# Two of a head's four causal masks move from TensorE to GpSimd

## The chip, the cores and the metric

One NeuronCore of a Trainium2 chip runs the whole kernel. The metric is the device time of one execution in microseconds. The engines are named as the profile names them: PE (TensorE matmul), PEld (its weight loads), DVE (VectorE), ACT (ScalarE), POOL (GpSimd) and SP (SyncE, which issues the DMAs).

## The reference

Attention with 4 x 8 heads, 576 positions and 64 features per head, and then two dense layers on the 2304 x 512 result.

```python
scores = scale * np.matmul(q, k.transpose(0, 1, 3, 2))
causal = np.triu(np.ones((S, S), dtype=bool), k=1)
cum = np.cumsum(np.maximum(s, 0.0), axis=-1)
bias = -(cum[:, :, :, None] - cum[:, :, None, :])
scores = np.where(causal, -1000000000.0, scores + np.minimum(bias, 0.0))
attn = np.exp(scores - max); attn = attn / (sum + 1e-09); out = attn @ v
h = x @ w_in;  x = (h - np.tanh(h)) @ w_out                    # first layer, d_ff 2048
h = x @ w_in;  x = (h * np.clip(h + 3, 0, 6) / 6) @ w_out      # second layer, d_ff 2048
```

## The kernel before, in words

**Stages.** The attention of 32 heads (16 pairs) runs to about 198 us, the first dense layer to about 600 us, the second to the end.

**A pair of heads** (`heads`) loads q and k (`lq`, `lk`), and splits each into a rounded high part and a rest: ACT makes the high q (`q1`, L421) and the high k for the second operand (`k2`, L433), DVE casts k (`kh`, L430), and GpSimd makes the two rests (`ql`, L427, and `kl`, L437). PE multiplies high parts for an upper bound on each row's scores (`mx`, L481), DVE reduces that to a maximum (`rd`, L490), and the maximum goes back through DRAM as extra rows of the q operand.

**The scores of a head** (`scores`) are transposed: keys on the partitions, queries along the free axis. Five key tiles are packed into four PSUM banks, c = 0 to 3 (`CHUNKS`), 256, 320, 512 and 512 columns wide. The function `st` (L575) issues a bank's matmuls in the order of `STEPS[c]`: `h` multiplies the 128-row operand with the rests, `l` the 68-row operand with the high parts, the bias and the maximum, and `m` multiplies the bf16 identity `identb` with a bf16 mask tile `maskT`, which adds -8e9 where the key is later than the query. Banks 0, 2 and 3 have such an `m`, 128, 192 and 2 x 128 columns wide (`MASKS`). ACT then takes the exponential of the whole bank into an SBUF tile `pt` (`ex`, L578; two tiles for each c), and PE multiplies it with the values (`pv`, L605, four groups per head in the order c = 0 to 3). A row of ones in the values gives the sum of the exponentials.

**What sets the order.** Nothing is scheduled at run time. `Plan` is a list scheduler in the host code: each operation has an engine, an estimated duration (`mm_us`, `vec_us`), a priority (`PRIO` plus a term that grows with the head), and buffers; the plan's start times give the order in which each engine's instructions are issued, and each engine then runs its own list strictly in that order, with semaphores between them. Constants of the plan are the latency after an operation (`LAT`) and a model of the DMAs (`DMA_US`, `DMA_KB_US`, `ISSUE`). Operations marked `port` (DVE and GpSimd work on two SBUF operands or in a copy) aren't planned beside each other, and each such GpSimd operation gets a dependence on the last such DVE operation of the plan.

**Around it.** While attention runs, ACT and DVE also turn the first 6 of 16 packed weight blocks of the first layer from 64-bit words into two rounded float parts (`rounded` and `convert`, L748 to L779, priority `conv`); the other 10 follow after attention, when their buffers come free (`close`). After every fourth pair GpSimd multiplies the batch's outputs with the reciprocal sums (`no`, L673), the last batch on DVE. The first layer's matmuls are L830 and L861, those of the second L1122 and L1198.

Of the kernel before, what the change touches and what calls it, by code (L numbers as in the profile page):

```python
# [15 lines left out]
ALU = mybir.AluOpType  # L16
# [8 lines left out]
SP = 640  # L25
# [12 lines left out]
CHUNKS = [  # L38
    [(0, 0, 256, 0)],
    [(0, 256, 320, 0)],  # L40
    [(4, 512, 64, 0), (1, 128, 448, 64)],
    [(3, 384, 192, 0), (2, 256, 320, 192)],
]
CW = [256, 320, 512, 512]

MASKS = [(1, 64, 128), None, (1, 0, 192), (2, 64, 128)]

STEPS = ["h0 l0 m", "h0 l0", "h1 l1 h0 l0 m", "h1 h0 l1 l0 m"]

MAXT = [[(2, 384, 0), (4, 576, 384)], [(3, 512, 0)], [(1, 256, 0), (0, 128, 256)]]  # L50
TINY, HUGE = (float(np.array([b], np.uint32).view(np.float32)[0]) for b in (0x38000000, 0x47F00000))
# [6 lines left out]

PRIO = {
# [3 lines left out]
}  # L65

# [40 lines left out]

class Plan:  # L110
    LAT = {"PE": 0.30, "ACT": 0.05, "DVE": 0.09, "POOL": 0.09, "V": 0.0}
    DMA_US, DMA_KB_US, ISSUE = 1.6, 220.0, 0.55

    def __init__(self):
        self.ops = []
# [23 lines left out]
    def schedule(self):  # L139
        wait, ready = {}, {}  # L140
        free = {}
# [10 lines left out]
        while done < len(self.ops):  # L152
# [6 lines left out]
            while frees and frees[0][0] <= t:  # L159
                _, _, b = heapq.heappop(frees)  # L160
                b.pool.free.append(b.t)
            for e in wait:
                while wait[e] and wait[e][0][0] <= t + 1e-9:
                    _, i, o = heapq.heappop(wait[e])
                    heapq.heappush(ready[e], (o.prio, i, o))
            again = True
            while again:
                again = False
                for e in ready:
# [25 lines left out]
                    o = chosen  # L195
# [21 lines left out]
                            heapq.heappush(frees, (b.end, id(b), b))  # L217
                    for n in o.next:
                        n.left -= 1
                        n.ready = max(n.ready, o.end)  # L220
                        if n.left == 0:
                            heapq.heappush(wait[n.eng], (n.ready, order[n], n))
                            if n.ready <= t:
                                heapq.heappush(events, t)
# [3 lines left out]

def mm_us(n, f32=False):

    return (4 * n / 2.4 + 6) / 1e3 if f32 else max(0.1, (n / 2.4 + (13 if n > 128 else 5)) / 1e3)


def vec_us(n, ghz, fixed):
    return (n / ghz + fixed) / 1e3
# [3 lines left out]
def kernel(  # L239
# [10 lines left out]
    nc = tc.nc  # L250
    plan = Plan()
# [43 lines left out]
    def r(b):  # L295
        return late[b.t] if isinstance(b.t, str) else b.t
# [99 lines left out]

    T = PRIO["T"]
    alloc_prev = [None, None]
# [158 lines left out]
    def scores(h, hh, t0, b1, b2, vf, deps, lv, xp, xb, bt, sds):  # L557
        def st(c, b):
# [13 lines left out]

            mms = [step(x) for x in STEPS[c].split()]
            for i, (o, w, x) in enumerate(mms):
                nc.tensor.matmul(o, w, x, start=(i == 0), stop=(i == len(mms) - 1), skip_group_check=True)  # L575

        def ex(c, b, pt):
            nc.scalar.activation(r(pt), r(b)[:, 0 : CW[c]], AF.Exp, scale=0.125)  # L578

        exs, pts, sts = [], [], []  # L580
        for c in range(4):
            b, pt = Buf(banks), Buf(ptp[c])
            us = sum(2 * mm_us(n) for _, _, n, _ in CHUNKS[c]) + (mm_us(MASKS[c][0] * MASKS[c][2]) if MASKS[c] else 0)
            so = plan.op("PE", us, lambda c=c, b=b: st(c, b), deps, [b1, b2, b], t0 + PRIO["st"] + PRIO["dst"] * c, name=f"st{h}_{c}")
            sts.append(so)
            exs.append(plan.op("ACT", vec_us(CW[c], 1.2, 165), lambda c=c, b=b, pt=pt: ex(c, b, pt), [so], [b, pt], t0 + PRIO["ex"] + PRIO["dst"] * c, name=f"ex{h}_{c}"))
            pts.append(pt)
        st_done[h] = sts
        po = [Buf(banks, greedy=True) for _ in range(2)]
# [21 lines left out]
        for c in range(4):  # L611
            us = sum(mm_us(n, True) for _, _, _, n, _ in segments(c))
# [24 lines left out]
        sd = plan.dma(sd_, 2, [ov1], own, t0 + PRIO["sd"], name=f"sd{h}")  # L637
        batch_sd.setdefault(bt, []).append(sd)
        if hh:
            so = plan.dma(lambda: nc.sync.dma_start(xp()[64:128], r(sg)[0:D, :]), 147, [sds[0], ov1], own + [xb], t0 + PRIO["so"], name=f"so{h}")  # L640
# [680 lines left out]
```

## Time and profile before

| | us |
|---|---|
| median of 3 runs (957.64 to 961.81) | 960.91 |
| the profiled execution, its own time | 957.06 |
| its span, first to last instruction | 955.3 |
| PE busy | 933.0 |
| DVE busy | 672.8 |
| ACT busy | 464.9 |
| GpSimd busy | 161.2 |

A busy time is the time in which an engine had at least one instruction under way. Matmuls are pipelined, so what one of them costs is read from the distance between its start and the next one's start, not from its own duration. A timeline row merges neighbours of one group: its columns are start, length, engine, line, operation, tiles, shapes, how many instructions, and in brackets the idle time ahead and what ended it.

### The profile page before, as it was taken

What the parts mean: (1) busy time and instruction counts of PE and PEld (TensorE: products, weight loads), DVE (VectorE), ACT (ScalarE), POOL (GpSimd) and SP (SyncE); (2) the same over time, 40 slices, a digit from 0 to 9 for tenths busy, and PEclk for the clock granted to TensorE, in tenths of its full rate; (3) what the DMA queues carried; (4) which work ended last, traced back from release to release, by engine and by line L of the source; (5) the groups of instructions that cost most, each with busy time, mean ns of one, the idle gap of its engine ahead of it and who ended that gap; (6) DMA issues with size and microseconds to landing.
All of it is one profiled execution on the core that took longest, in us unless ns stands there. A gap on an engine that the chain in (4) does not pass through costs nothing.

```text
span 955.3 us, 14956 instructions
## 1 busy us (share of the span) xinstructions
PE 933.0 (98%) x5560; PEld 831.9 (87%) x5560; DVE 672.8 (70%) x1107; ACT 464.9 (49%) x714; POOL 161.2 (17%) x106
## 2 busy tenths in 40 slices
PE   3999999999999999999999999999999999999998
PEld 3777777778878888998888888999999999999997
DVE  7887778789988766685676834657776577764763
ACT  2677677754534443444344333444454444544441
POOL 8344755600000000012222222000000000000000
PEclk9999999999999999999999999999999999999999
DMA  5667786796236448555546681776886767877672
GB/s 121 189 176 186 212 208 204 186 331 208 98 128 223 176 156 282 177 179 197 198 155 207 228 292 46 244 229 208 250 307 228 232 199 258 298 235 223 210 224 97
DMA packets 70521, 195.91 MB, mean 205 GB/s; under 512 B 11634, under 2 KB 20338, under 8 KB 69168
## 3 DMA queue, kind: packets, MB, share of 16 engines
q1 hardware_dynamic: 70448, 194.95, 64.3%
q8 instruction: 44, 0.72, 0.3%
q14 instruction: 29, 0.24, 0.1%
HBM read 143.75 MB, written 44.09 MB: 197 GB/s over the span
## 4 chain that ended last, share of the span: by engine, by line
PE 92%; DVE 3%; DMA 2%; ACT 1%; issue 1%; SPq 0%; DVEq 0%; ACTq 0%
PE bank L830 20%; PE bank L861 20%; PE pair L1198 19%; PE pair L1122 18%; PE bank L605 8%; PE bank L575 5%; DVE junk L490 1%; PE wide L481 1%; DMA tq<-in_q_dram 1%; PE bank L481 1%; DMA Q<-mdram 0%; DMA rdram<-rb 0%; ACT w L778 0%; DVE K L430 0%; DVE f_w L1142 0%
## 5 line engine op out<-in xcount | busy, mean ns | idle before, releaser
L861 PE MATMUL bank<-gg,w 128*128 128x512 f32 (+1 forms) x960 | 234.3, 368 | 0.5 <-ACT gg L849 0.3
L830 PE MATMUL bank<-xx,w 128*128 128x512 f32 (+1 forms) x960 | 233.2, 368 | 0.0
L861 PEld LDWEIGHTS bank<-gg,w 128*128 128x128 f32 x960 | 170.1, 189 | 30.9 <-ACT gg L849 1.3
L830 PEld LDWEIGHTS bank<-xx,w 128*128 128x128 f32 x960 | 170.5, 188 | 30.4
L1122 PE MATMUL pair<-op_w,w 128*128 128x384 f32 x648 | 118.0, 334 | 0.6 <-DVE f_w L1142 0.6
L841 ACT ACTIVATE g<-bank 128x512 f32<-128x512 f32 (+1 forms) x80 | 44.5, 556 | 148.2 <-PE bank L830 124.9
L1198 PE MATMUL pair<-w,op_W 128*128 128x256 f32 x918 | 115.1, 283 | 0.0
L1122 PEld LDWEIGHTS pair<-op_w,w 128*128 128x128 f32 x648 | 112.4, 188 | 1.2 <-DVE f_w L1142 0.9
L1198 PEld LDWEIGHTS pair<-w,op_W 128*128 128x128 f32 x918 | 112.8, 192 | 0.0
L605 PE MATMUL bank<-pt,vf 128*66 128x320 f32 (+4 forms) x448 | 106.9, 360 | 0.3 <-ACT pt L578 0.3
L851 POOL TENSOR_TENSOR gg<-g,gg 128x512 fp32r<-128x512 f32 x32 | 47.5, 1486 | 345.0 <-ACT gg L849 307.8
L845 DVE TENSOR_TENSOR g<-bank,g 128x512 f32<-128x512 f32 (+1 forms) x80 | 50.8, 635 | 64.4 <-ACT g L841 63.7
L575 PE MATMUL bank<-Q,K 128*128 128x320 f32 (+9 forms) x384 | 88.7, 352 | 1.6 <-ACT stage L628 1.1
L575 PEld LDWEIGHTS bank<-Q,K 128*128 128x128 f32 (+3 forms) x384 | 63.5, 186 | 23.3 <-ACT stage L628 1.7
L578 ACT ACTIVATE pt<-bank 128x512 f32<-128x512 f32 (+2 forms) x128 | 62.4, 500 | 33.3 <-PE bank L575 31.6
L849 ACT ACTIVATE gg<-g 128x512 fp32r<-128x512 f32 (+1 forms) x80 | 47.0, 587 | 43.4 <-DVE g L845 35.0
L490 DVE CUSTOM_DVE_ANT_0 junk<-bank,maskA 128x512 bf16<-128x512 f32 (+2 forms) x96 | 45.0, 469 | 20.6 <-PE bank L481 13.2
L605 PEld LDWEIGHTS bank<-pt,vf 128*66 128x66 f32 x448 | 50.5, 141 | 6.7 <-ACT pt L578 0.5
L427 POOL TENSOR_TENSOR Q<-tq,Q 64x1152 fp32r<-64x1152 f32 (+1 forms) x17 | 42.4, 2494 | 53.6 <-PE bank L575 9.0
L490 DVE CUSTOM_DVE_ANT_0 junk<-wide,maskA 128x384 bf16<-128x384 f32 x64 | 41.8, 653 | 10.0 <-PE wide L481 5.4
L437 POOL TENSOR_TENSOR K<-tq,K 64x1152 fp32r<-64x1152 f32 (+1 forms) x17 | 42.8, 2519 | 20.3 <-ACT stage L628 6.3
L1198 PE MATMUL pair<-w,op_B 128*128 128x256 f32 x342 | 44.1, 283 | 0.0
(305 smaller groups left out, 1303.3 us busy)
## 6 DMA issues: line engine op xcount, KB each, us to landing
w<-wdram SPq DMA_DIRECT2D x149, 512.0 KB
wdram<-cv SPq DMA_DIRECT2D x56, 512.0 KB
raw_c<-in_w_dram SPq DMA_DIRECT2D x11, 1024.0 KB
raw_b<-in_w_dram SPq DMA_DIRECT2D x11, 1024.0 KB
raw_a<-in_w_dram SPq DMA_DIRECT2D x12, 512.0 KB
vf<-in_v_dram SPq DMA_DIRECT2D x16, 330.0 KB
rb<-rdram SPq DMA_DIRECT2D x8, 576.0 KB
xdram<-xb SPq DMA_DIRECT2D x16, 288.0 KB
```

Source lines behind the costliest of these rows:

```text
L490: nc.vector.tensor_tensor_reduce(out=junk[0:rr, 0:w], in0=r(b)[0:rr, col : col + w], in1=maskA[0:rr, m0 : m0 + w], scale=1.0, scalar=-3.0e ...
L575: nc.tensor.matmul(o, w, x, start=(i == 0), stop=(i == len(mms) - 1), skip_group_check=True)
L578: nc.scalar.activation(r(pt), r(b)[:, 0 : CW[c]], AF.Exp, scale=0.125)
L605: nc.tensor.matmul(r(po[bank])[0:DV, oc : oc + n], r(vf)[:, j, hh, :], r(pts[c])[:, col : col + n], start=(j == 0), stop=(bank == 0 and c ...
L830: nc.tensor.matmul(r(ps)[:, 0:w], wt[:, c, :], x(c)[:, 0:w], start=(part == 0 and c == 0), stop=(part == 2 and c == NCC - 1),)
L841: nc.scalar.activation(r(g)[:, 0:w], r(ps)[:, 0:w], AF.Tanh)
L845: nc.vector.tensor_sub(x, r(ps)[:, 0:w], x)
L849: gho = plan.op("ACT", vec_us(w, 1.2, 205), lambda: nc.scalar.activation(r(gh)[:, 0:w], r(g)[:, 0:w], AF.Copy), [m, to_gg], [g, gh], base)
L851: glo = plan.op("DVE" if beside else "POOL", vec_us(w, 0.96, 155) if beside else vec_us(w, 0.44, 160), lambda: (nc.vector if beside else n ...
L861: nc.tensor.matmul(r(acc[e])[:, 0:w], a[:, es], bb[:, 0:w], start=f, stop=l)
L1122: nc.tensor.matmul(bank(k)[:, l], w[hw][:, l, kc], r(x)[:, hx, kc], start=(i in (1, 5, 2) and j == 0 and kc == 0), stop=(j == 2 and kc == ...
L1198: nc.tensor.matmul(r(c[k])[:, m * 256 : (m + 1) * 256], r(x)[:, hx, l, m * P : (m + 1) * P], w[hw][:, l], start=(i == order[chain_first[k] ...
```

## The change

For banks 0 and 3 the matmul `m` goes away. After the exponential, a GpSimd `affine_select` in place on the `pt` tile writes 0 where the key is later than the query: on 128 columns of bank 0, and on two blocks of 128 columns (stride 192) of bank 3. The `pv` group of that bank now waits for GpSimd instead of ACT. The `select` isn't marked `port`. Bank 2 keeps its mask matmul.

The same diff changes the plan: a new set of priorities (`se` is new; `lq`, `k2`, `kl`, `rd`, `ex`, `sd` and `conv` differ), other constants for DMAs, other estimates for matmuls, and a successor on the same engine is ready as soon as the engine is free instead of after the latency. So the order of all engines' instructions may differ in all stages, while the work of the instructions themselves differs only in the masks.

```diff
-STEPS = ["h0 l0 m", "h0 l0", "h1 l1 h0 l0 m", "h1 h0 l1 l0 m"]
+STEPS = ["h0 l0", "h0 l0", "h1 l1 h0 l0 m", "h1 h0 l1 l0"]
-PRIO = {
-    "lq": -82.46, "q1": -19.46, "kh": -21.99, "k2": 46.29, "q2": 73.66, "ql": -97.67, "kl": 7.77, "cu": 15.04,
-    "mx": -26.19, "rd": -24.46, "mf": -46.57, "mo": 141.04, "mi": -48.74, "lv": -41.09, "st": 6.08, "ex": -101.91,
-    "pv": 10.88, "ov": -102.07, "sd": 106.8, "so": -143.57, "no": 47.74, "conv": 159.69, "T": 6.53, "dst": 0.25,
-}
+PRIO = {'se': -112.8, 'lq': -87.52, 'q1': -19.46, 'kh': -21.99, 'k2': 4.61, 'q2': 73.66, 'ql': -97.67, 'kl': 45.94, 'cu': 15.04, 'mx': -26.19, 'rd': -32.68, 'mf': -46.57, 'mo': 141.04, 'mi': -48.74, 'lv': -41.09, 'st': 6.08, 'ex': -100.38, 'pv': 10.88, 'ov': -102.07, 'sd': 98.56, 'so': -143.57, 'no': 47.74, 'conv': 181.65, 'T': 6.53, 'dst': 0.25}
-    DMA_US, DMA_KB_US, ISSUE = 1.6, 220.0, 0.55
+    DMA_US, DMA_KB_US, ISSUE = 1.9, 230.0, 0.62
-                        n.ready = max(n.ready, o.end)
+                        n.ready = max(n.ready, free[o.eng] if o.eng == n.eng != "SP" else o.end)
 def mm_us(n, f32=False):
-    return (4 * n / 2.4 + 6) / 1e3 if f32 else max(0.1, (n / 2.4 + (13 if n > 128 else 5)) / 1e3)
+    return (4 * n + 20) / 2.4e3 if f32 else (n + 32) / 2.4e3
+        def zero(c, pt):
+            k, _, n = MASKS[c]
+            a = r(pt)[:, 0 : k * 192].rearrange("p (k n) -> p k n", k=k)[:, :, 0:n]
+            return nc.gpsimd.affine_select(
+                out=a, in_=a, pattern=[[0, k], [1, n]], compare_op=ALU.is_ge, fill=0.0, base=0, channel_multiplier=-1,
+            )
-            us = sum(2 * mm_us(n) for _, _, n, _ in CHUNKS[c]) + (mm_us(MASKS[c][0] * MASKS[c][2]) if MASKS[c] else 0)
+            us = sum(2 * mm_us(n) for _, _, n, _ in CHUNKS[c]) + (MASKS[c][0] * MASKS[c][2] / 2.4e3 + 0.03 if "m" in STEPS[c] else 0)
+            if c in (0, 3):
+                k, _, n = MASKS[c]
+                exs[c] = plan.op("POOL", (k * n + 170) / 1e3, lambda c=c, pt=pt: zero(c, pt), [exs[c]], [pt], t0 + PRIO["se"] + PRIO["dst"] * c, name=f"se{h}_{c}")
```

## Rows read from the trace of the kernel before

**Rows 1.** The page: busy us, share and instructions by engine; clock tenths by slice.

```profile
PE 933.0 (98%) x5560; PEld 831.9 (87%) x5560; DVE 672.8 (70%) x1107; ACT 464.9 (49%) x714; POOL 161.2 (17%) x106
PEclk9999999999999999999999999999999999999999
```

**Rows 2.** The page: the chain that ended last, shares by line.

```profile
PE bank L830 20%; PE bank L861 20%; PE pair L1198 19%; PE pair L1122 18%; PE bank L605 8%; PE bank L575 5%; DVE junk L490 1%; PE wide L481 1%; DMA tq<-in_q_dram 1%; PE bank L481 1%; DMA Q<-mdram 0%; DMA rdram<-rb 0%; ACT w L778 0%; DVE K L430 0%; DVE f_w L1142 0%
```

**Rows 3.** Busy time by stretch: us and instructions per engine, clock, DMA share, GB/s.

```profile
core 0: us, PE busy (x) PEld busy (x) DVE busy (x) ACT busy (x) POOL busy (x), PEclk, DMA share, GB/s
...
25.00:50.00 25.00, 24.14 (x141) 18.05 (x141) 20.61 (x75) 16.47 (x29) 9.05 (x4) 1.00 0.71 188
125.00:150.00 25.00, 23.87 (x154) 18.60 (x153) 17.57 (x57) 17.45 (x34) 16.19 (x9) 1.00 0.84 209
...
250.00:275.00 25.00, 24.54 (x107) 19.61 (x107) 23.14 (x28) 11.84 (x15) 0.00 (x0) 1.00 0.26 84
...
25.00:200.00 175.00, 173.00 (x1096) 135.11 (x1096) 140.03 (x422) 126.80 (x242) 92.04 (x41) 1.00 0.75 198
```

**Rows 4.** Timeline of PE in steady attention, 79 to 86.5 us.

```profile
79.29 0.60 PE L605 MATMUL bank<-pt,vf 128*66 128x256 f32 x2
...
80.45 0.64 PE L575 MATMUL bank<-Q,K 128*128 128x256 f32 x2
80.93 0.23 PE L575 MATMUL bank<-maskT,identb 128*128 128x128 bf16 x1
81.00 1.04 PE L605 MATMUL bank<-pt,vf 128*66 128x64 f32 x6
...
82.17 1.03 PE L605 MATMUL bank<-pt,vf 128*66 128x192 f32 x4
...
85.85 0.64 PE L575 MATMUL bank<-Q,K 128*128 128x256 f32 x2
```

**Rows 5.** Timeline of PE, 194 to 195 us: a mask of bank 3.

```profile
194.21 0.28 PE L575 MATMUL bank<-maskT,identb 128*128 128x256 bf16 x1
194.33 1.03 PE L605 MATMUL bank<-pt,vf 128*66 128x192 f32 x4
```

**Rows 6.** The chain in order of time (start, us, what), in the second layer.

```profile
713.15 2.08 PE pair L1122 x12
715.24 2.15 PE pair L1198 x18
```

**Rows 7.** Groups of GpSimd by line and shape: busy us, mean ns, idle before.

```profile
L851 POOL TENSOR_TENSOR gg<-g,gg 128x512 fp32r<-128x512 f32 x32 | 47.5, 1486 | 345.0 <-ACT gg L849 307.8 <-PE bank L861 37.1
L437 POOL TENSOR_TENSOR K<-tq,K 64x1152 fp32r<-64x1152 f32 x15 | 40.0, 2669 | 20.2 <-ACT stage L628 6.3 <-DVE K L430 5.0 <-ACT pt L578 4.2
...
L360 POOL TENSOR_SCALAR_AFFINE_SELECT maskT<-maskT 128x128 bf16<-128x128 bf16 x2 | 0.5, 295 | 0.0
...
L360 POOL TENSOR_SCALAR_AFFINE_SELECT maskT<-maskT 128x64 bf16<-128x64 bf16 x1 | 0.2, 240 | 0.1
```

**Rows 8.** Timeline of ACT, 72 to 84 us: two exponentials of one head.

```profile
75.87 0.38 ACT L578 ACTIVATE pt<-bank 128x256 f32<-128x256 f32 x1 [1.33 <-PE bank L575]
...
79.13 0.60 ACT L578 ACTIVATE pt<-bank 128x512 f32<-128x512 f32 x1 [0.24 <-DVE wy L759]
```

**Rows 9.** Waits of PE from 22 to 200 us: total us, times, longest.

```profile
PE bank L605 <- ACT pt L578: 0.3, 1, 0.3
```

**Rows 10.** Timeline of GpSimd, 125 to 200 us.

```profile
177.47 2.65 POOL L427 TENSOR_TENSOR Q<-tq,Q 64x1152 fp32r<-64x1152 f32 x1 [1.89 <-DVE wy L759]
```

**Rows 11.** Timeline of DVE, 140 to 275 us: weight conversion and the first layer's start.

```profile
178.41 2.25 DVE L779 TENSOR_TENSOR w<-wy,w 128x512 fp32r<-128x512 f32 x1 [1.17 <-ACT w L778]
...
196.91 0.69 DVE L779 TENSOR_TENSOR w<-wy,w 128x512 fp32r<-128x512 f32 x1
...
203.28 0.69 DVE L845 TENSOR_TENSOR g<-bank,g 128x512 f32<-128x512 f32 x1 [2.60 <-ACT g L841]
```

**Rows 12.** The chain in order of time, early in the first layer.

```profile
252.28 1.24 DVE w L779
253.55 1.17 ACT wy_b L752
255.35 1.22 DVE wy L757
257.09 1.22 DVE wy L759
```

## The prediction

> **What bounds the kernel now.** I read the page's busy shares first. PE is busy for 933.0 of 955.3 us, DVE for 70%, GpSimd for 17%, and the clock row is at its top digit in every slice, the 2.4 GHz level [rows 1]. The chain that ended last lies on PE lines almost throughout, with 5% on L575 (scores with their masks) and 8% on L605 (`pv`) [rows 2]. The question is whether the masks' own stage has the same limit. From 25 to 200 us PE is busy for 173.0 of 175 us, and DVE for 140.0, ACT for 126.8, GpSimd for 92.0 [rows 3]. One head follows the other after 5.40 us (first score matmul at 80.45, next at 85.85) [rows 4]. So in this stage TensorE time is elapsed time, and an engine that takes work over has 83 us free as long as nobody has to wait for it.
>
> **What is removed.** 64 matmuls with a mask tile. The row of a matmul shows 0.23 or 0.28 us, most of it pipeline, so I take the distance to the next start. The 128-column mask starts at 80.93 and the next matmul at 81.00: 0.07 us [rows 4]. The 256-column mask starts at 194.21 and the next one at 194.33: 0.12 us [rows 5]. A head loses 0.07 + 0.12 = 0.19 us, 32 heads 6.1 us. A check from other rows: in the second layer twelve 384-column matmuls take 2.08 us and eighteen 256-column ones 2.15 us [rows 6], 0.173 and 0.119 us each. So 128 columns are worth 0.054 us and a matmul has 0.011 us on top; that gives 0.065 + 0.119 = 0.184 us a head and 5.9 us in all. I take 6.0. Their weight loads need no term: PEld is busy for 135 of 175 us of the stage [rows 3], and the load goes with its matmul.
>
> The Trainium skill ("TensorE: Matmul & The Clock Gate", section "Back-to-back issue gap") puts the distance of warm matmuls at columns / 2.4 ns plus 2.5 ns, which would be 0.056 + 0.109 us a head and 5.3 us in all, an estimate by that page. The trace's 0.119 us for 256 columns is above it and decides.
>
> **What is added.** Two `affine_select` a head on GpSimd. The trace has this instruction on bf16 alone: 0.295 us for 128 columns and 0.240 for 64 [rows 7], so 0.055 us per 64 columns, and by the same slope 0.405 us for 256. The tiles are f32 now, which no row shows. The dearest neighbour is a GpSimd subtract with two f32 inputs, 1.486 us for 512 columns [rows 7]; in proportion 0.37 and 0.74 us. Below the bf16 price I see no reason to go, since the fixed part stays. A select has one input, so I take the bf16 end: 0.70 us a head, 22 us in all; the dear end is 1.11 and 36 us. With that GpSimd would be busy for 114 to 128 us of a stage of some 169, so as a total it is hidden at either end.
>
> What counts is when a select is done. `pv` of a bank now waits for the select, and what is queued behind it on PE waits too, for PE runs its list strictly in order. In the trace the first exponential of a head ends at 75.87 + 0.38 = 76.25 and its `pv` starts at 79.29, 3.0 us later; that of bank 3 ends at 79.13 + 0.60 = 79.73 and its `pv` starts at 82.17, 2.4 us later [rows 4, 8]. An idle GpSimd needs 0.3 or 0.4 us of that, and PE sees nothing. But the subtracts `ql` and `kl` take 2.67 us each [rows 7] and can't be interrupted. A select of bank 3 right behind the start of one would be done 2.67 + 0.41 = 3.08 us after the exponential, 0.6 too late; bank 0's at 2.67 + 0.30 = 2.97 is just in time. Two subtracts in a pair's 10.8 us make that an arrival in the first 0.6 us of one: 1.2 of 10.8, 11%, with 0.3 us lost on average. 32 x 0.11 x 0.3 = 1.1 us. The plan knows the subtracts and puts other PE work ahead in part of these cases, so I take half, 0.5 us. Today PE waits for an exponential once in the whole stage, 0.3 us [rows 9]; such a spot becomes later by a select, 0.4 us. Together 0.9 us; bounds are zero and the price of the third rival.
>
> **What is moved.** Priorities and the plan's constants reorder all lists, on POOL and SP too: `kl` goes down, `k2` and `lq` go up, conversions (`conv`) move 22 units down, so they fall behind the last heads' work, and DMA issues are planned further apart. No instruction is added by that. What can be won or lost is PE's idle time: 0.86 us from 25 to 50, 1.13 from 125 to 150, 0.46 from 250 to 275 [rows 3]. I take zero, with 2.4 us to either side. On ACT nothing new waits; `pt` tiles live longer by a select, and there are two for each bank.
>
> **Sum.** -6.0 + 0.9 = -5.1 us. Against the profiled execution this is 957.06 - 5.1 = 952.0, with a span of 950.2. That execution lies 3.9 us below the median of the runs, and the 5.1 us come off either, so 960.9 - 5.1 = 955.8 us.
>
> **Rivals.**
> First: the new order also closes idle time ahead of PE, the 0.86 + 1.13 + 0.46 us named above. For it: these gaps are waits for a late operation, not for work. Against it: the plan that left them was made the same way. Time: 955.8 - 2.4 = 953.4.
>
> Second: the gain is given back when the first layer starts. The last weight conversion of the attention stage ends at 196.91 + 0.69 = 197.60, with the stage itself [rows 11]. A stage that is 6 us shorter has 6 us less DVE time; if DVE has no way to close up, 6 us of work slide behind it. There DVE has one hole of 2.60 us, ahead of 203.28 [rows 11], and then 23.14 us of work in 25 while the chain runs through conversions [rows 3, 12]. 6.0 - 2.6 = 3.4 us would land on PE: 955.8 + 3.4 = 959.2. Against it: DVE has 35 us idle in the stage [rows 3]. What would push the case further is that a GpSimd instruction holds up DVE: a subtract of a conversion took 2.25 us at 178.41, against 0.69 at 196.91, while a GpSimd subtract ran from 177.47 to 180.12 [rows 10, 11]. 64 selects of 0.35 us on average could hold DVE for up to 22 us, less than its 35 - 6 = 29 us that would be left, so I add nothing for it. The Trainium skill says the same as a rule ("SBUF — State Buffer", section "Who interferes with whom"): DVE with two SBUF inputs and a GpSimd instruction that reads SBUF lock each other out for a whole instruction. By that rule the selects may also be held by DVE, which speaks against the change; the row of 2.25 us agrees with it.
>
> Third, the slower side: GpSimd's queue becomes the clock of `pv`. The mechanism is the 2.67 us subtract ahead of a select, this time not in 11% of the cases but by rule, because what releases a subtract (the end of a head's scores, the copies of ACT) comes shortly ahead of that head's exponentials. Each of the 32 subtracts then makes one select late by 0.3 us on average (9.6 us) up to 0.6 (19). It decides from 6.0 / 32 = 0.19 us per subtract on, where the gain is gone. Time: 960.9 - 6.0 + 9.6 = 964.5 up to 974, its middle 969. For it: GpSimd's load rises to some 70%, and f32 may be dearer than bf16. Against it: 2.4 to 3.0 us of room.
>
> **How the numbers follow.** The forecast has 0.50, the first rival 0.15, the second 0.20, the third 0.15. About 0.5% (4.8 us, so 956.1 and 965.7) is what a measurement of this kernel can tell from no change. Faster: two thirds of the forecast, 0.34, and the first rival, 0.15: 0.49. Slower: most of the third, 0.13. The rest, 0.38, is no difference. The range goes from 951.5 (the first rival, with the 2 us by which runs differ) to 963.0 (the second rival, with DVE making up nothing, 955.8 + 6.0, and one us of those 2); it leaves out the third rival and little else.
>
> **What would show it.** In the profile after: 64 matmuls fewer on L575's mask row; a head every 5.2 us instead of 5.40; attention's end near 192 us instead of 198; 64 selects of 0.30 and 0.41 us; `pv` waiting for GpSimd for about 1 us in all, in few places; PE's busy time near 927. Wrong would be: many waits of L605 for the select (third rival), PE waits from 245 to 280 us above the present 0.5 (second), a select of 0.4 and 0.7 us, or idle time early in the attention that differs by more than 2.4 us, which would mean that the new order matters more than the masks.

## The result, and the profile after

| | us | ratio to before, 95% interval |
|---|---|---|
| before, median of 7 runs beside it (957.26 to 961.81) | 959.08 | |
| changed kernel, median of 7 runs (964.43 to 968.51) | 965.60 | 1.0067 [1.0046, 1.0088] |
| changed kernel, profiled execution | 968.51 | |

The change makes the kernel slower by 6.4 us, a ratio of 1.0067 on 959; 955.8 us was predicted, in a range from 951.5 to 963.0. Below, a ratio is turned into microseconds in the same way, (ratio - 1) x 959. The profiled execution is the longest of the seven, with a mean granted clock of 0.997; the runs of this kernel at 0.999 to 1.0 take 964.4 to 966.5 us.

The page, busy time and instructions of each engine; the line of before is in [rows 1].

```profile
PE 935.4 (97%) x5496; PEld 829.5 (86%) x5496; DVE 687.6 (71%) x1107; ACT 463.4 (48%) x714; POOL 189.4 (20%) x170
```

The 64 matmuls are gone (5560 to 5496), and GpSimd has 64 instructions and 28.2 us more. (A head has three mask matmuls, in banks 0, 2 and 3, and two of them go; the four of the title are its banks, of which bank 1 never had one.) PE's busy time, forecast near 927 us, rose by 2.4 instead. The chain that ended last, by engine and by line, against [rows 2]:

```profile
PE 86%; DVE 5%; POOL 4%; DMA 2%; issue 1%; ACT 1%; SPq 0%; POOLq 0%; DVEq 0%; ACTq 0%
PE bank L836 20%; PE bank L867 20%; PE pair L1204 19%; PE pair L1128 18%; PE bank L611 5%; PE bank L571 3%; DVE junk L486 2%; POOL Q L423 2%; POOL K L433 1%; PE wide L477 1%; POOL pt L579 1%; DMA K<-cdram 1%; DMA tq<-in_k_dram 1%; DVE wy L763 0%; PE bank L477 0%
```

GpSimd was not on the chain before. Now it has 4% of it, and more with the two subtracts, L423 (`ql`) and L433 (`kl`), than with the selects (L579). The stretches answer [rows 3] (columns as there):

```profile
250.00:275.00 25.00, 25.00 (x112) 20.71 (x111) 22.63 (x29) 11.11 (x14) 0.00 (x0) 1.00 0.27 93
25.00:200.00 175.00, 165.86 (x976) 125.24 (x976) 134.53 (x404) 117.72 (x226) 115.10 (x98) 0.99 0.73 187
```

From 25 to 200 us PE is busy for 165.9 us instead of 173.0. The first layer loses nothing at its start: 112 matmuls in 250 to 275 us, 107 before. The end of the attention on PE's timeline, the changed kernel and then the kernel before, where L836 and L830 are the first layer:

```profile
207.81 1.91 PE L611 MATMUL bank<-pt,vf 128*66 128x128 f32 x7
209.31 0.86 PE L836 MATMUL bank<-xx,w 128*128 128x512 f32 x2
```

```profile
197.66 1.10 PE L830 MATMUL bank<-xx,w 128*128 128x512 f32 x3
```

The first layer begins at 209.3 us, before at 197.7: 11.6 us later, and the span of the profile is 11.5 us longer (966.8 against 955.3). So the loss is in the attention. What PE (then PEld) waited for from 15 to 300 us, in total us, times, longest; [rows 9] shows before:

```profile
PE bank L611 <- POOL pt L579: 6.6, 16, 0.9
PE wide L477 <- DVE mrow L515: 3.3, 1, 3.3
PE wide L477 <- DVE Mt L486: 1.7, 3, 1.4
PE wide L477 <- DMA K<-cdram: 1.0, 1, 1.0
...
PEld bank L611 <- POOL pt L579: 12.6, 22, 1.0
```

L611 is `pv`. It waits for a select 16 times, its weight load 22 times (partly the same events, so the sums are not added). Why the selects are late is on GpSimd's timeline, two pairs of heads from 59 to 78 us:

```profile
59.64 2.63 POOL L423 TENSOR_TENSOR Q<-tq,Q 64x1152 fp32r<-64x1152 f32 x1 [0.26 <-DVE Mt L486]
62.34 0.93 POOL L579 TENSOR_SCALAR_AFFINE_SELECT pt<-pt 128x256 f32<-128x256 f32 x1
63.35 2.65 POOL L433 TENSOR_TENSOR K<-tq,K 64x1152 fp32r<-64x1152 f32 x1
66.07 0.66 POOL L579 TENSOR_SCALAR_AFFINE_SELECT pt<-pt 128x128 f32<-128x128 f32 x2
...
70.88 2.64 POOL L423 TENSOR_TENSOR Q<-tq,Q 64x1152 fp32r<-64x1152 f32 x1 [3.36 <-DMA mdram<-mrow]
73.59 0.81 POOL L579 TENSOR_SCALAR_AFFINE_SELECT pt<-pt 128x256 f32<-128x256 f32 x1
74.48 2.65 POOL L433 TENSOR_TENSOR K<-tq,K 64x1152 fp32r<-64x1152 f32 x1
77.20 0.66 POOL L579 TENSOR_SCALAR_AFFINE_SELECT pt<-pt 128x128 f32<-128x128 f32 x2
```

Most pairs look like these: `ql`, at once the 256-column select of the odd head's bank 3, at once `kl`, at once the 128-column select of the next even head's bank 0. A select with nothing ahead has a bracket with idle time; these have none. What that does to PE and ACT (first PE, then ACT's exponentials):

```profile
74.45 1.08 PE L611 MATMUL bank<-pt,vf 128*66 128x192 f32 x4 [0.41 <-POOL pt L579]
77.66 0.60 PE L611 MATMUL bank<-pt,vf 128*66 128x256 f32 x2
```

```profile
70.32 1.18 ACT L574 ACTIVATE pt<-bank 128x512 f32<-128x512 f32 x2 [0.16 <-PE bank L571]
74.04 0.69 ACT L574 ACTIVATE pt<-bank 128x256 f32<-128x256 f32 x2
```

Bank 3's exponential is ready at 71.50, its select starts at 73.59, and `pv` starts at 74.45, 0.05 us after the select's end; before, such a `pv` started 2.4 us behind its exponential and found it done [rows 4, 8]. Over the 64 selects the wait behind the exponential is 1.1 us on average, 69 us in all. In that time GpSimd is busy with subtracts for 52 us, with normalisations for 9 and with other selects for 4, and idle for 4. 30 of the 64 have a subtract ahead and wait 0.5 to 3.2 us, 18 of these 1.9 or more, and 26 `pv` groups start less than 0.2 us after their select.

### The profile page after: what moved, and what is told of

The parts are those of the page before. It is cut to its first block, busy times and chain, and to the rows that moved or that the text cites. A ratio compares the mean times of both kernels' runs of the same rounds, so it can differ in the third digit from the quotient of the medians.

```text
span 966.8 us, 14890 instructions
## 1 busy us (share of the span) xinstructions
PE 935.4 (97%) x5496; PEld 829.5 (86%) x5496; DVE 687.6 (71%) x1107; ACT 463.4 (48%) x714; POOL 189.4 (20%) x170
## 4 chain that ended last, share of the span: by engine, by line
PE 86%; DVE 5%; POOL 4%; DMA 2%; issue 1%; ACT 1%; SPq 0%; POOLq 0%; DVEq 0%; ACTq 0%
PE bank L836 20%; PE bank L867 20%; PE pair L1204 19%; PE pair L1128 18%; PE bank L611 5%; PE bank L571 3%; DVE junk L486 2%; POOL Q L423 2%; POOL K L433 1%; PE wide L477 1%; POOL pt L579 1%; DMA K<-cdram 1%; DMA tq<-in_k_dram 1%; DVE wy L763 0%; PE bank L477 0%
## 5 line engine op out<-in xcount | busy, mean ns | idle before, releaser
L867 PE MATMUL bank<-gg,w 128*128 128x512 f32 (+1 forms) x960 | 210.6, 368 | 1.4 <-ACT gg L855 1.4
L836 PE MATMUL bank<-xx,w 128*128 128x512 f32 (+1 forms) x960 | 210.1, 368 | 0.0
L836 PEld LDWEIGHTS bank<-xx,w 128*128 128x128 f32 x960 | 168.3, 189 | 30.2
L1128 PEld LDWEIGHTS pair<-op_w,w 128*128 128x128 f32 x672 | 116.8, 188 | 0.1
L611 PE MATMUL bank<-pt,vf 128*66 128x320 f32 (+4 forms) x448 | 100.8, 371 | 7.2 <-POOL pt L579 6.6
L1204 PE MATMUL pair<-w,op_W 128*128 128x256 f32 x738 | 93.1, 283 | 0.0
L1204 PEld LDWEIGHTS pair<-w,op_W 128*128 128x128 f32 x738 | 90.7, 192 | 0.0
L611 PEld LDWEIGHTS bank<-pt,vf 128*66 128x66 f32 x448 | 53.3, 143 | 32.2 <-POOL pt L579 12.6
L571 PE MATMUL bank<-Q,K 128*128 128x320 f32 (+9 forms) x384 | 73.2, 324 | 0.8 <-POOL K L433 0.8
L571 PEld LDWEIGHTS bank<-Q,K 128*128 128x128 f32 (+3 forms) x384 | 58.9, 186 | 11.7 <-POOL K L433 1.2
L1204 PE MATMUL pair<-w,op_B 128*128 128x256 f32 x432 | 55.7, 283 | 0.0
L1204 PEld LDWEIGHTS pair<-w,op_B 128*128 128x128 f32 x432 | 53.6, 192 | 0.0
L423 POOL TENSOR_TENSOR Q<-tq,Q 64x1152 fp32r<-64x1152 f32 (+1 forms) x17 | 42.6, 2504 | 27.0 <-PE bank L571 12.3
```

The source lines that it names most:

```text
L423: return nc.gpsimd.tensor_sub(r(b2)[0][64:128, a], r(tq)[0:64, a], f32(r(b1)[0])[0:64, a, 0:S])
L611: nc.tensor.matmul(r(po[bank])[0:DV, oc : oc + n], r(vf)[:, j, hh, :], r(pts[c])[:, col : col + n], start=(j == 0), stop=(bank == 0 and c ...
L836: nc.tensor.matmul(r(ps)[:, 0:w], wt[:, c, :], x(c)[:, 0:w], start=(part == 0 and c == 0), stop=(part == 2 and c == NCC - 1),)
L867: nc.tensor.matmul(r(acc[e])[:, 0:w], a[:, es], bb[:, 0:w], start=f, stop=l)
L1128: nc.tensor.matmul(bank(k)[:, l], w[hw][:, l, kc], r(x)[:, hx, kc], start=(i in (1, 5, 2) and j == 0 and kc == 0), stop=(j == 2 and kc == ...
L1204: nc.tensor.matmul(r(c[k])[:, m * 256 : (m + 1) * 256], r(x)[:, hx, l, m * P : (m + 1) * P], w[hw][:, l], start=(i == order[chain_first[k] ...
```

## Experiments

All ratios are to the kernel before on the same chips. In the diffs only the lines that carry the edit stand. Every list of instructions comes out of the plan, and two kernels can be compared strictly only where the plan gives the same lists. masks_off, same_order, mask_twice, light_on and light_off have the lists of the kernel before; short_sub, short_norm and short_both have those of the changed kernel; short_off and short_both_off have those of off_path. In plan_only, off_path, select_first, quarters and one_each the plan has other operations or dependences and makes another order: some 70 to 105 of PE's 1000 operations stand elsewhere than in the changed kernel.

### Is it the masks, the plan, or the wait?

**masks_off**: the kernel before without the two masks, nothing in their place, order unchanged.

```diff
-STEPS = ["h0 l0 m", "h0 l0", "h1 l1 h0 l0 m", "h1 h0 l1 l0 m"]
+STEPS = ["h0 l0", "h0 l0", "h1 l1 h0 l0 m", "h1 h0 l1 l0"]
```

> The kernel before without the mask matmuls of banks 0 and 3, and with nothing in their place: the later keys stay in these banks, so part of the mask is left out. The plan's durations are kept, so every engine's list is that of before. All theories: the first term of the prediction, 64 matmuls at 0.067 and 0.121 us, 6.0 us less, so 953 us. If matmuls with the mask were hidden beside something, less than 3 us would come off. No new wait of PE is expected.

957.14 us, ratio 0.9969 [0.9951, 0.9988]: 3.0 us, about half of what the matmuls' length gives.

**plan_only**: the changed kernel with its new priorities and constants, but with both masks back on TensorE and no select.

```diff
-STEPS = ["h0 l0", "h0 l0", "h1 l1 h0 l0 m", "h1 h0 l1 l0"]
+STEPS = ["h0 l0 m", "h0 l0", "h1 l1 h0 l0 m", "h1 h0 l1 l0 m"]
-            if c in (0, 3):
+            if c in ():
```

> The kernel after with the mask matmuls back on PE and no select: new priorities and constants of the plan alone. Theory 1 (queue: selects stand behind the 2.65 us subtracts on GpSimd, and pv waits): within 2.5 us of before, 957 to 962. Theory 2 (order: the new plan itself costs the time): the plan must cost the 6.5 us of the change plus the 6.0 us that the masks give, so 970 to 972.

958.48 us, 0.9979 [0.9964, 0.9994]: the new plan by itself gains 2.0 us. It beats both kernels.

**off_path**: the changed kernel, its selects writing to a tile of their own; `pv` waits for ACT.

```diff
-                out=a, in_=a, pattern=[[0, k], [1, n]], ...
+                out=zt[:, 0 : k * n].rearrange("p (k n) -> p k n", k=k), in_=a, ...
-                exs[c] = plan.op("POOL", (k * n + 170) / 1e3, ...
+                plan.op("POOL", (k * n + 170) / 1e3, ...
```

> The kernel after, but each select writes to a tile of its own that nobody reads, and pv waits for the exponential as before: GpSimd has the same 64 selects, PE doesn't wait for them, and the mask of banks 0 and 3 is left out of the result. Theory 1 (queue): 952 to 956, no wait of PE for GpSimd in pv. Theory 2 (order): 964 to 967. Theory 3 (load: 30 us more of GpSimd work make the subtracts late and hold up DVE through the shared reads of SBUF, whoever waits for the selects): 962 to 966, with waits of the score matmuls for the subtract of k.

957.55 us, 0.9959 [0.9943, 0.9974]. The same 64 selects with the same load on GpSimd, and the time is 10.4 us below the changed kernel's (1.0067 against 0.9959, with 2.5 us to either side from the two intervals). So neither the new plan nor the selects' work costs the time. That the waits of `pv` do is what is left, with one doubt: the order is near the changed kernel's but not the same, and the 10.4 us hold what that is worth. The next run has no such doubt.

**same_order**: the kernel before with its own plan; the select is issued right behind its exponential.

```diff
             nc.scalar.activation(r(pt), r(b)[:, 0 : CW[c]], AF.Exp, scale=0.125)
+            if c in (0, 3):
+                zero(c, pt)
```

> The kernel before with the selects in the place of the two mask matmuls and no new plan: the select is issued right behind its exponential, every other list is that of the kernel without these masks (957.1 us). It tells the price of the waits from that of a new order. The prediction's sum (subtracts meet a select by chance, 2.4 to 3.0 us of room): 0.9 us, so 958. If the subtracts stand ahead of the selects by rule and the room is not enough: 962 to 968, and pv waits for GpSimd at one select per subtract.

964.19 us, 1.0053 [1.0036, 1.0071]: 8.1 us above masks_off, whose order on PE, ACT, DVE and SP is the same. What differs is the 64 selects and that `pv` waits for them. So the loss is not a matter of the new plan either. PE's waits, 15 to 300 us, and a piece of the timelines of ACT, GpSimd and PE:

```profile
PE bank L614 <- POOL pt L585: 6.5, 8, 1.8
```

```profile
187.35 0.88 ACT L578 ACTIVATE pt<-bank 128x512 f32<-128x512 f32 x2
```

```profile
188.52 2.98 POOL L437 TENSOR_TENSOR K<-tq,K 64x1152 fp32r<-64x1152 f32 x1 [1.71 <-DVE wy L766]
191.58 0.99 POOL L585 TENSOR_SCALAR_AFFINE_SELECT pt<-pt 128x256 f32<-128x256 f32 x2
```

```profile
192.37 2.05 PE L614 MATMUL bank<-pt,vf 128*66 128x192 f32 x8 [1.80 <-POOL pt L585]
```

Fewer and longer waits than in the changed kernel. Both exponentials are done by 188.23, but `kl` stands ahead of their two selects. It itself waits for DVE until 188.52, 0.6 us of that with the first select's input ready, then runs for 2.98 us, and PE idles for 1.80 us. In this kernel, too, 30 of the 64 selects have a subtract ahead.

### Is it what stands ahead of the select?

**select_first**: in the changed kernel, `ql` is made to depend on bank 3's select of an earlier head (2p - 3), so that the select goes first.

```diff
-            oql.append(plan.op("POOL", pool, ql, [oq1[-1], a2] + ...
+            oql.append(plan.op("POOL", pool, ql, [oq1[-1], a2, selects.get(2 * p - 3)] + ...
```

> The kernel after with one more dependence: the subtract ql of pair p starts after the select of bank 3 of head 2p-3, the head whose scores free its buffers. Theory 1 (queue): these 14 selects no longer wait 1.9 us for a subtract, nor does the chain of pv groups behind them: 956 to 960, and the wait of pv for GpSimd falls from 19 us (PE and its loads) to under 8. Theory 2 and 3: 964 to 968, since no work is taken away.

966.26 us, 1.0054 [1.0031, 1.0076]. The waits for selects fell and the time did not:

```profile
PE bank L838 <- DVE xx L822: 5.0, 2, 2.5
PE bank L613 <- POOL pt L580: 3.9, 7, 1.5
```

Waits for selects: 3.9 us in 7 instead of 6.6 in 16, and the attention ends at 199.8. But at the first layer's start PE waits 5.0 us for inputs that DVE makes, a wait that the changed kernel doesn't have, and there the granted clock is at 0.50 from 203.0 to 209.9 us, which takes some 2 more. Of the 9.5 us by which the attention ends sooner, 7.4 are gone after the first 25 matmuls of the first layer. With another order and these two in it, the run says little about the selects.

**quarters**: in the changed kernel, each subtract cut into four pieces with a select allowed between them.

```diff
-                return nc.gpsimd.tensor_sub(r(b2)[0][64:128, a], r(tq)[0:64, a], f32(r(b1)[0])[0:64, a, 0:S])
+                return nc.gpsimd.tensor_sub(r(b2)[0][64:128, a, c], r(tq)[0:64, a, c], f32(r(b1)[0])[0:64, a, c])
```

> The kernel after with each GpSimd subtract (ql, kl) cut into four of a quarter of the columns, 0.7 us each, planned one by one, so that a select can slip in between. The same work, some 0.1 us more for each piece (10 us more of GpSimd in all). Theory 1 (selects wait for a 2.65 us instruction that can't be interrupted): the wait of pv for GpSimd falls from 19 us to under 6, and the time to 957 to 961. Load of GpSimd or its locks as the cause: more GpSimd time, so 966 to 969.

986.73 us, 1.0288 [1.0266, 1.0310], a miss. GpSimd's groups (busy us, mean ns) and PE's waits:

```profile
L423 POOL TENSOR_TENSOR Q<-tq,Q 64x288 fp32r<-64x288 f32 x60 | 50.9, 868 | 13.6 <-PE bank L578 5.5 <-PE bank L484 3.9 <-DVE rb L670 1.8
```

```profile
PE bank L578 <- POOL K L433: 16.0, 3, 8.2
PE bank L618 <- POOL pt L586: 7.9, 11, 1.5
```

A quarter costs 0.87 us (one of `kl` 0.84), not 2.65 / 4 = 0.66, so four take 3.4 us. `kl` now comes late for the score matmuls (L578), 16.0 us in 3 waits. Cutting work moved the lateness from the selects to the rests of q and k. Its mean granted clock is 0.987 against 0.999 in plan_only: it is at half for 23.9 us of the time up to 225 us, 14.6 of them with PE at work, which is some 7 of the 27.6 us.

**short_sub** and its control **short_off**: the changed kernel and off_path, with 64 of 576 columns in each subtract from the third pair on.

```diff
+            cw = S if p < len(seconds) else 64
-                return nc.gpsimd.tensor_sub(r(b2)[0][64:128, a], r(tq)[0:64, a], f32(r(b1)[0])[0:64, a, 0:S])
+                return nc.gpsimd.tensor_sub(r(b2)[0][64:128, a, 0:cw], r(tq)[0:64, a, 0:cw], f32(r(b1)[0])[0:64, a, 0:cw])
```

> The changed kernel, but from the third pair of heads on the two GpSimd subtracts ql and kl work on 64 columns of each head instead of 576 (the low parts of Q and K keep stale values there, so the output is not the reference's); the order on every engine is that of the changed kernel, and every select and every wait stays. Theory (a pv waits because its select stands behind a 2.65 us subtract in GpSimd's list): the time falls to the level of off_path, 955 to 958 us, and PE's waits for GpSimd's selects nearly go, from 16 times to 3 or fewer. Rival (the extra engine between exponential and pv costs the time by itself, through the hand-over and the selects that VectorE holds up): 963 to 966 us, with as many waits as before.

> The control of short_sub: off_path (selects that write to a tile of their own, nobody waits for them) with the same short subtracts. What it gains over off_path (957.6) is what shorter subtracts give for another reason, such as VectorE being held up less: expected 0 to 2 us, so 955.5 to 957.6. By the theory short_sub comes out within 1.5 us of this kernel; by the rival 6 us or more above it.

short_sub 960.14 us, 1.0001 [0.9982, 1.0019]; short_off 956.91, 0.9962 [0.9948, 0.9977]. Shorter subtracts take 6.3 us off the changed kernel and nothing off the control (0.9959 before). So they are the larger part of the loss, and 3.7 us remain. The profile of short_sub, GpSimd from 100 us on:

```profile
100.66 1.41 POOL L680 TENSOR_TENSOR xb<-xb,rb 128x576 f32<-128x576 f32 x1 [1.91 <-DVE Mt L487]
102.02 0.41 POOL L580 TENSOR_SCALAR_AFFINE_SELECT pt<-pt 128x256 f32<-128x256 f32 x1
102.52 0.45 POOL L423 TENSOR_TENSOR Q<-tq,Q 64x128 fp32r<-64x128 f32 x1
```

The subtract is down to 0.45 us, and what stands ahead of the select here is a normalisation, which itself had waited 1.91 us for DVE, the last 0.6 of it with the select's input ready (its exponential ended at 100.05).

**short_norm**, **short_both** and the control **short_both_off**: the changed kernel with GpSimd's 12 normalisations on 64 columns; with both kinds of work short; and off_path with both short.

```diff
-                return (nc.vector if last else nc.gpsimd).tensor_mul(x, x, r(rb)[:, c * S : (c + 1) * S])
+                if last:
+                    return nc.vector.tensor_mul(x, x, r(rb)[:, c * S : (c + 1) * S])
+                return nc.gpsimd.tensor_mul(x[:, 0:64], x[:, 0:64], r(rb)[:, c * S : c * S + 64])
```

> The changed kernel with GpSimd's 12 normalisations of xb on 64 of their 576 columns (the rest stays unnormalised, so the output is not the reference's), subtracts whole, order unchanged. If the normalisations ahead of selects cost the 3.2 us that short_sub left: 962.4 us, 3.2 below the changed kernel. If they cost nothing and the rest is the hand-over to a third engine: 965 to 966 us.

> The changed kernel with both kinds of GpSimd work short: subtracts on 64 columns from the third pair on, normalisations on 64 columns. All 64 selects and all waits of pv for them stay. Theory (the whole loss is work ahead of selects in GpSimd's list): within 1 us of short_both_off, about 956.5 us, TensorE waiting for a select at most once. Rival (part of the loss is the hand-over exponential, select, pv itself): 959 to 960 us.

> The control of short_both: selects write to a tile of their own and nobody waits for them, both kinds of work short. Expected 956 us (short_off was 956.9; the short normalisations may take another 0 to 1 us off VectorE's held-up instructions).

| changed kernel with | us | ratio | against the changed kernel |
|---|---|---|---|
| nothing else | 965.60 | 1.0067 [1.0046, 1.0088] | |
| short_sub | 960.14 | 1.0001 [0.9982, 1.0019] | -6.3 |
| short_norm | 962.97 | 1.0024 [1.0013, 1.0036] | -4.1 |
| short_both | 956.61 | 0.9963 [0.9949, 0.9977] | -10.0 |
| short_both_off | 954.03 | 0.9943 [0.9929, 0.9957] | -11.9 |

The two parts add up: 6.3 + 4.1 = 10.4, and together 10.0. The first four kernels of the table have one order, so 10.0 us are what the shortening gives. It takes 1.5 us off the control as well (0.0016 x 959, off_path against short_both_off); the rest, 8.5 us, is the price of the work ahead of selects in GpSimd's list. With both short, all 64 selects and all 64 dependences of `pv` are still there, and what is left against the control is 0.0020 x 959 = 1.9 us, with an interval that nearly reaches zero. This is the hand-over and the control's other order together. In the two profiles the control's attention even ends 5.3 us sooner (first layer at 192.2 against 197.5), and the first layer takes 2.5 of them back. short_both's waits of PE, and its selects:

```profile
PE bank L612 <- POOL pt L580: 0.8, 2, 0.6
```

```profile
L580 POOL TENSOR_SCALAR_AFFINE_SELECT pt<-pt 128x256 f32<-128x256 f32 x32 | 13.8, 430 | 34.1 <-ACT pt L575 34.0
L580 POOL TENSOR_SCALAR_AFFINE_SELECT pt<-pt 128x128 f32<-128x128 f32 x32 | 10.7, 334 | 40.9 <-ACT pt L575 37.0 <-DVE Mt L487 2.6 <-DMA xdram<-xb 0.6
```

GpSimd now idles ahead of the selects until ACT is done (34.0 and 37.0 us). In the changed kernel these idle times were 4.0 and 20.8:

```profile
L579 POOL TENSOR_SCALAR_AFFINE_SELECT pt<-pt 128x256 f32<-128x256 f32 x32 | 17.8, 555 | 5.0 <-ACT pt L574 4.0
L579 POOL TENSOR_SCALAR_AFFINE_SELECT pt<-pt 128x128 f32<-128x128 f32 x32 | 11.7, 365 | 23.3 <-ACT pt L574 20.8 <-DVE K L426 1.4
```

**one_each**: a select only where it seldom stands behind a subtract (bank 0 of odd heads, bank 3 of even ones), masks for the rest.

```diff
+        own_bank = 0 if hh else 3
-            if c in (0, 3):
+            if c == own_bank:
```

> The changed kernel, with a select only in bank 0 of odd heads and in bank 3 of even heads (in its profile these 32 seldom stand behind a subtract: mostly 0.07 to 0.7 us after the exponential), and the mask matmul kept for the other 32. If the waits come by rule from where the two subtracts stand in each pair of heads: TensorE waits for GpSimd at most 4 times, and the time is the new plan's 958.5 less half of the masks' 3 us, 957 us (955.5 to 958.5). If they fall by chance on any select: half of the changed kernel's 8 us stays, 961 to 962 us.

961.01 us, 1.0008 [0.9994, 1.0022]. The waits are as expected if they come by rule (2.0 us in 3), but the time is the one expected if they fall by chance. With half of the selects the planner made another order, so this run does not isolate the rule; it says only that this mixture doesn't beat plan_only.

### Why are the masks worth 3 us and not 6?

**light_on** and **light_off**: the kernel before, and masks_off, with a broadcast of the reciprocal sums of a quarter of the bytes.

```diff
-                nc.sync.dma_start(dst, src[i : i + 1].broadcast_to([D, NCC, S]))
+                nc.sync.dma_start(dst, src[i : i + 1, 0:1].broadcast_to([D, 1, S]))
```

> The kernel before, its masks on PE, but the broadcast of the reciprocal sums after each batch moves a quarter of the bytes (0.3 instead of 1.2 MB for each of four batches); all heads of a batch are normalised with the first ones' sums, so the normalisation is partly left out. The same order. It is the base for the next kernel. PE hardly waits for DMAs before, so 957 to 960 by all theories.

> The same light broadcast, and the mask matmuls of banks 0 and 3 left out as in the kernel without masks. Theory DMA (the 6.0 us of PE were there, and 3 of them went into loads of k and q rows that stood behind the broadcast's 1.2 MB): 5 to 6.5 us under the light kernel with masks, 951 to 954, and no wait of PE for K<-cdram and Q<-Q in the stretches behind a broadcast. If the masks are worth only 3 us by themselves: 3 us under it.

light_on 956.02, 0.9967 [0.9954, 0.9981]; light_off 952.87, 0.9938 [0.9919, 0.9957]. The masks are worth 2.8 us here too, so late DMAs behind the broadcast are not what takes the other half, though the broadcast costs 3.2 us by itself.

**mask_twice**: the kernel before with each of the 64 mask matmuls issued twice.

```diff
+STEPS = ["h0 l0 m m", "h0 l0", "h1 l1 h0 l0 m", "h1 h0 l1 l0 m m"]
```

> The kernel before with the mask matmul of banks 0 and 3 issued twice (the second adds the same large negative numbers again, so the result is the same), order unchanged. Taking the 64 matmuls away gave 3 us where their length is 6.0 us. If TensorE sets the pace and only something just behind it took the other half of the gain, adding them costs the whole length: +6.0 us, 965 us. If half of the heads hide such a matmul behind another wait, both ways: +3 us, 962 us.

961.83 us, 1.0019 [1.0006, 1.0032]: +1.8 us. So by the medians neither direction gives 6. The traces of before, masks_off and mask_twice have one order on PE, so their starts can be compared matmul by matmul. Over six heads without a wait, from 55.0 to 87.6 us of before, masks_off gets 1.00 us ahead and mask_twice falls 1.05 us behind: 0.17 us a head each way, 5.3 to 5.6 us for 32 heads. So the length was nearly right, and what differs is where it ends up. The first layer of mask_twice begins here (before's row, 197.66, stands in the first section):

```profile
202.18 1.10 PE L830 MATMUL bank<-xx,w 128*128 128x512 f32 x3
```

In the profile the doubled masks thus cost 4.5 us at the end of the attention, 4.9 in the span (960.2 against 955.3), and little hides them. The medians differ by less because before's runs beside mask_twice spread from 957.0 to 964.8 us, with a median of 959.8, and its trace is of an execution of 957.06; mask_twice's spread only from 961.1 to 962.4. What before's median holds above its trace no run here shows. That light_on spreads only from 955.7 to 957.1 would fit DMAs behind the broadcast.

In the other direction the gain meets waits. The first layer of masks_off begins at 197.73 us, no sooner than before's, after DMAs that came late:

```profile
PE bank L575 <- DMA Q<-Q: 2.0, 1, 2.0
PE wide L481 <- DMA K<-cdram: 1.3, 1, 1.3
```

Behind the first of these the granted clock is at half for a while, which takes 1.7 us more (last section). In light_off neither wait is there, and the first layer begins 3.3 us sooner than in light_on (193.2 against 196.5); PE idles 1.9 us more ahead of it, most of that for one DMA near 34 us, and 0.7 us is lost again early in the first layer.

With the new plan the attention ends 5.4 us sooner in off_path than in plan_only (last start 193.2 against 198.6), but the time is only 1.9 us less. The first layer's stretch, plan_only and then off_path, two microseconds of the latter, and its longest wait there:

```profile
250.00:300.00 50.00, 47.65 (x207) 38.18 (x206) 46.08 (x59) 21.77 (x31) 0.00 (x0) 1.00 0.37 125
```

```profile
250.00:300.00 50.00, 46.88 (x199) 37.97 (x198) 45.00 (x59) 22.55 (x31) 0.00 (x0) 0.97 0.38 120
```

```profile
260.00:262.00 2.00, 2.00 (x6) 1.50 (x6) 1.97 (x4) 0.00 (x0) 0.00 (x0) 0.50 0.03 8
```

```profile
PE bank L868 <- ACT gg L856: 3.1, 2, 2.1
```

207 matmuls in one, 199 in the other, at 0.227 us each: 1.8 us lost again here. PE waits 2.1 us for ACT, which has a weight conversion ahead of `gg`, and then the clock is at half; DVE is busy for 45 to 46 of the 50 us. The chain of off_path in this stretch (start, us, what) runs through weight conversions too:

```profile
267.01 1.21 DVE wy_c L764
268.23 0.60 DVE gg L858
268.83 1.15 DVE wy_c L766
```

That is the second rival's mechanism, with a loss of clock on top.

## Why the prediction was wrong

**The bound** held: PE sets the pace of the attention. Of the loss only a part shows as PE idle time, 9.1 us instead of 2.0 from 25 to 200 us, while the attention ends 11.6 us later with 64 matmuls fewer.

**The removed work**, -6.0 us, was nearly right as a length (5.3 to 5.6 us of matmul work) and wrong as a gain. It is worth 3.0 us in the old plan, 1.9 in the new one (2 us to either side), and doubling it costs 1.8, all by the ratios above. The step that failed is taking 173.0 of 175 us busy for "TensorE time is elapsed time": a change of 3% of the stage meets waits that the profile of before left almost no trace of, for DMAs during the attention and for conversions behind it. That profile was also of an execution 2 us below the median of 959.08. That the 0.12 us of [rows 5] fits was luck: for 24 of the 32 masks of bank 3 in that trace the next start follows after 0.04 us, and the matmul that starts there is longer instead. One row's distance is not the price; the shift of all later starts is.

The rule cited from the Trainium skill ("TensorE: Matmul & The Clock Gate", section "Back-to-back issue gap") would have put the length at 5.3 us, and the traces' 5.3 to 5.6 are nearer to that than to the 6.0 from rows. That section gives the rule as the gap of an isolated matmul and says that in a stream of weight loads and matmuls it is too low at 128 columns, some 81 ns, and too high at 512, some 131 ns. Here the measurement decides against both figures: two 128-column masks in a row start 67 ns apart (mask_twice), and 20 matmuls of 512 columns with their loads take 4.53 us (off_path, from 249.84 us on), 227 ns each.

**The added work.** The price of a select was right: 0.29 and 0.41 us where nothing holds it, f32 as the bf16 of [rows 7]. The step that failed is the arrival, 11% of the heads with 0.3 us each, cut to half because "the plan knows the subtracts": +0.9 us. Measured is +8.1 (old order, against masks_off) to +10.4 (new plan, against off_path). 11% of the heads are three or four late selects; in the changed kernel 30 of the 64 have a subtract ahead, and 26 `pv` groups start right behind their select. The third rival had the mechanism: the subtract ahead by rule, at 9.6 us and more, with a chance of 0.15 and outside the range. Its lowest time, 964.5, is close to the 965.6 measured, in part by luck, since it counts the full 6.0 us as gained. Three things were missing from the estimate.
- More than one long instruction can stand ahead, and the one at the head of the list may itself be waiting for an input that has nothing to do with the select (0.6 us of the case at 188.52 above), so 2.67 us is no upper end: the longest waits are 3.2 us in the changed kernel and 4.0 in same_order. In the changed kernel the waiting is the small part: of the 69 us GpSimd idles for 4.
- The 12 normalisations of 1.47 us were not counted at all; they cost about 4 us.
- The room of 3.0 and 2.4 us was read at one head. It was typical (the medians over the heads of before are 2.9 and 2.5), but 13 of the 64 had less than 2.0, and the subtract with the select's own time uses up even the typical room. `ql` is released by the end of a head's score matmuls (12.3 of 27.0 us of its idle time end with L571), the work that releases the exponentials too: what the third rival said.

The hand-over itself was taken at 0.4 us; 1.9 were measured, with the interval and the other order named above.

**The lock** of DVE and GpSimd was counted at nothing, and no run shows that it cost time by itself. The Trainium skill ("SBUF — State Buffer", section "Who interferes with whom") says that one of the two blocks the other for a whole instruction; the traces agree, with selects of up to 0.97 us instead of 0.28 to 0.41 and 14.8 us more of DVE busy time. off_path has these too and is 3.9 us faster than before.

**The moved work**, 0 with 2.4 us to either side: -2.0 us, inside the bound and close to the first rival's value. **The second rival** did not appear in the changed kernel, whose attention ends too late for it, and appears where the attention ends sooner (off_path, short_both_off).

The sum as measured: -2.0 for the plan, -1.9 for the masks in it, +10.4 for the waits: +6.5, against the +6.4 of the result. It must agree, since each term is the step from one of four kernels to the next; it shows where the time is, and the runs of one order (8.1 and 10.0 us) show why.

## What to carry to other kernels

Work that moves to an engine which runs its list in order costs what stands ahead of it there, and not its own duration: before you move a step of 0.3 us onto a critical chain, list every long instruction of the new engine and ask which event releases each. If the same event releases both the long instruction and the new step's input, expect the collision as the rule. And where an engine is busy for 99% of a stage, a removed length need not come back as time: here a half (3.0 of 6.0 us) or a third (1.9) did. A run without that work shows it before anything is put in its place.

## What the runs showed of the hardware

**A pause of one or two microseconds can be followed by half of TensorE's clock.** In the changed kernel's profile PE idles 1.03 us for a DMA up to 147.98, and the granted clock (the column ahead of the DMA share) then falls:

```profile
146.00:148.00 2.00, 0.97 (x9) 0.81 (x7) 1.05 (x3) 1.12 (x2) 1.93 (x4) 1.00 1.04 224
148.00:150.00 2.00, 2.00 (x10) 1.59 (x11) 1.65 (x9) 0.73 (x2) 1.41 (x2) 0.80 0.74 178
150.00:152.00 2.00, 2.00 (x8) 1.13 (x7) 0.52 (x5) 0.30 (x1) 1.32 (x1) 0.50 0.95 251
152.00:154.00 2.00, 2.00 (x12) 1.35 (x10) 0.00 (x0) 0.45 (x2) 0.07 (x1) 0.85 0.51 156
```

0.50 is the 1.2 GHz level. The lost clock is 0.20 x 2 + 0.50 x 2 + 0.15 x 2 = 1.7 us, more than the pause of 1.03. masks_off shows the same after its 2.0 us wait for Q<-Q, with 0.50 and 0.67 in the next four microseconds, and off_path after its 2.1 us wait for `gg`. It does not follow every such pause: PE idles 1.1 us up to 141.0 in before and 1.8 us up to 192.4 in same_order, and the clock stays at 1.00. Which pause is followed by it is not shown.

**A GpSimd subtract has a fixed part**: 1152 columns 2.65 us, 288 columns 0.84 to 0.87, 128 columns 0.45 to 0.49. Between 128 and 288 columns that is 0.38 us for 160, between 288 and 1152 it is 1.80 us for 864; at no width at all 0.15 to 0.25 us would be left, an estimate from these.
